# Seven block products for one more second product of a two-MoE kernel, with W_out's factors made while it is decoded

## The chip, the cores and the metric

The kernel runs on one core of a Trainium2 chip. The metric is the device time of one execution in microseconds; the time before is the median of three runs. Engines are called PE (TensorE: matmul, with PEld for its weight loads), DVE (VectorE), ACT (ScalarE), POOL (GpSimd) and SP (SyncE, which issues the DMAs).

## The reference

Windowed attention (4 batches, 8 heads, 576 positions, head size 64, window 128) gives x of 2304 tokens by 512. Two feed-forward blocks follow, called MoE here, each with its own W_in (512 by 2048) and W_out (2048 by 512):

```python
def _moe_ref(x, w_in, w_out):
    h = x @ w_in
    g = h * np.cos(h)
    return (g @ w_out).astype(np.float32)

def _moe2_ref(x, w_in, w_out):
    h = x @ w_in
    neg, pos = h <= -1.0, h >= 1.0
    g = np.where(pos, h, np.where(neg, 0.0, (h + 1.0) ** 2 / 4.0))
    return (g @ w_out).astype(np.float32)
```

All values are float32. The weights reach the chip as raw 64-bit words, which the kernel decodes to float32.

## The kernel before, in words

**Numbers.** Each float32 operand of a matmul is split in a high and a low part (`hi` by an ACT copy, `lo` by a DVE subtraction, `sub_lo`, L295). A product of two operands is three matmuls: high by high, high by low, low by high.

**Stages.** Attention runs first; its last rounds overlap the start of the first MoE. Tokens go in three chunks of 768, and a half chunk (384 columns, `HT`) is the width of most matmuls. The stages in PE's order are attention, then (0,0), (0,1), (0,2) of the first MoE and (1,0), (1,1), (1,2) of the second. In (0,0) weights are decoded as they are used (`first_weights`, L715).

**First products.** From (0,1) on, h = x·W_in is made by Strassen's scheme: seven block products in place of eight, for each of eight pairs p of 128-column blocks of W_in. The factors of W_in (A11, A12, S1 to S4, A22) are sums of its blocks, made once (`first_sums`, L339), stored to DRAM (`fd`) and loaded by each chunk (`stream`, L854). The factors of x (B11 to T4) are made by `prep` (L390). `product` (L866) is one block product, six matmuls of 384 columns. The PSUM results are joined: `snapshot` (L881) is an ACT copy out of a bank on which PE goes on adding, and `join` (L886) is a DVE add. `act` (L898) makes g of h.

**Second products, two ways.** In (0,1), (0,2) and (1,0) y = g·W_out is the classic eight block products: `contract` (L938) is six matmuls, called for 8 pairs, 2 halves and 4 blocks of 128 outputs, so 384 matmuls a chunk. W_out lies in SBUF as sixteen tiles `W` (`wo`), split in high and low. In (1,1) and (1,2) `deep` (L999) uses the seven products here as well: it first makes all h and g of the chunk (8 pairs, 7 products each), combines g's blocks (`combine`, L1067, four DVE subtractions for a pair), splits them (`halved`, L1055, seven a pair) and then runs 7 times 8 blocks (`block`, L1023) of six matmuls, 336 a chunk. The factors M1 to M7 of W_out come from DRAM (`fo`).

**Where W_out's factors come from, before.** `second_weights` (L686) decodes the second MoE's weights from 262 us on, a pair each 31 us. W_out's decoded tiles go to DRAM (`wd`, 16 stores of 256 KB). In (1,0) they are loaded again and split to the `wo` tiles (L1160 to L1166). From 520 us on `second_factors` (L977) stores M1, M2 and M4 from these tiles, loads W_out's pairs from `wd` a second time, makes the sums for M3, M5, M6 and M7 and stores them.

**PSUM in `deep`.** There are eight banks: two each in `ha` (a step's running cell, by p's parity), `hb` (M2's result and M4's), `cs` and `zs`. For each pair PE's order is M1(p), M7(p-1), M2(p), M4(p-1), M6(p), M3(p-1), M5(p), written by `step` (L1092) and the loop behind it. M1, M6 and M7 are summed on one bank with a snapshot behind each; M4 has a bank of its own and is joined with M7's snapshot.

**What orders the work.** PE's order is that in which the code issues it. For ACT, DVE, POOL and SP a planner (`Plan`, L106; `order`, L142) simulates the kernel with a table of operation lengths (`COST`, L58 to L72: the length for which the engine is held, and the latency until a successor may start), gives each operation a latest start from the PE order, and writes each engine's order out at compile time. `after=` holds an operation back to a planned time. Buffers with a `queue` name are handed out in the order of their rank. The chip then runs each engine's list in order, with semaphores.

Of the kernel before, what the change touches and what calls it, by code (L numbers as in the profile page):

```python
# [39 lines left out]
OUT_FROM, OUT_STEP = 520.0, 12.0  # L40
W2_FROM, W2_STEP = 262.0, 31.0
EARLY = 2
SUM_FROM, SUM_STEP = 175.0, 15.6
# [8 lines left out]
U_BUFS = 2  # L52
UP_BUFS = 2
# [52 lines left out]
class Plan:  # L106
# [35 lines left out]
    def order(self):  # L142
# [25 lines left out]
        for tag in ("Q", "split", "raw", "pair", "half"):  # L168
# [89 lines left out]
def attention_moe_moe_kernel(  # L258
# [19 lines left out]
    wd = [dram.tile([128, 512], F32, name=f"wd{f}") for f in range(NF)]  # L278
# [367 lines left out]
    def moes():  # L646
# [3 lines left out]
        wd_res = [Res() for _ in range(NF)]  # L650
        wo = [[None] * NF for _ in range(2)]
# [10 lines left out]
        plan = Plan({"s": S_BUFS, "Q": Q_BUFS, "B": 14, "W": NF, "ld": LD_BUFS, "wu": U_BUFS, "so": SO_BUFS, "up": UP_BUFS, "split": N_SPLIT},  # L662
# [23 lines left out]
        def second_weights():  # L686

            def load_and_decode(j, u, ap, after):
                raw = Buf("ld", lambda: two.tile([128, 512], mybir.dt.int64, tag="ld", name=nm("wst"), bufs=LD_BUFS), "raw")
                op("S", "512", lambda: SP.dma_start(raw.t, w2[j // 2, j % 2]), writes=[raw], after=after)  # L690
                decode(raw, u, ap)

            for p in range(NP):
                s = Buf("up", pair_tile, "pair")
                start = W2_FROM + W2_STEP * p
                for f in (2 * p, 2 * p + 1):
                    load_and_decode(2 * f, s, lambda s=s, f=f: half_u(s.t, f), start)
                    t = Buf("so", part_tile)
                    c, i = (slice(256, 512), 3) if f % 2 else (slice(0, 512), 0)
                    w = c.stop - c.start  # L700
                    op("A", f"hi{w}", lambda t=t, s=s, f=f, c=c, w=w: ACT.copy(t.t[:, 0, 0:w], half_u(s.t, f)[:, c]),
                       reads=[s], writes=[t])
                    op("D", f"tt{w}", lambda t=t, s=s, f=f, c=c, w=w: sub_lo(
                        DVE, t.t[:, 1, 0:w], half_u(s.t, f)[:, c], t.t[:, 0, 0:w]), reads=[s], writes=[t])
                    op("S", str(w), lambda t=t, p=p, i=i, w=w: move(fd[1][p][i], t.t[:, :, 0:w]),
                       reads=[t], writes=[fac[1][p][i]])
                    a = Buf("wu", lambda: two.tile([128, 512], F32, tag="wu", name=nm("wu"), bufs=U_BUFS), "half")
                    load_and_decode(2 * f + 1, a, lambda a=a: a.t, start)
                    op("S", "256", lambda a=a, f=f: SP.dma_start(wd[f], a.t), reads=[a], writes=[wd_res[f]])
                first_sums(op, 1, p, s, lambda: Buf("so", part_tile), lambda i, p=p: fac[1][p][i])  # L710
# [4 lines left out]
        def first_weights(j):  # L715
# [5 lines left out]
            if h:  # L721
                u = Buf("wu", lambda: two.tile([128, 512], F32, tag="wu", name=nm("wu"), bufs=U_BUFS))
                ap = lambda: u.t
                wo[0][f] = w = Buf("W", lambda: big("W", NF, "wo"))
            else:
                if f % 2 == 0:
                    wi_u[p] = Buf("W", lambda: big("W", NF, "up", F32, (128, 4, 256))) if f < 12 else Buf("up", pair_tile)
# [58 lines left out]
        def mm_b(i, f):  # L786
# [4 lines left out]
            def go():  # L791
# [3 lines left out]
                for d in range(KD):  # L795
                    s = slice(d * 128, d * 128 + 128)
                    for k, (a, x) in enumerate(((0, 0), (0, 1), (1, 0))):
                        PE.matmul(y_of[i][d], lhsT=wo[0][f].t[:, a, s], rhs=part(x),  # L798
# [3 lines left out]
            return op("PE", f"b{w}", go, reads=[wo[0][f], *gs], writes=[bank[t] for t in tags])  # L802
# [3 lines left out]
        def evict(m, c, y, d, o, w, res):  # L806
            e = "DA"[turn[0] % 2]
# [32 lines left out]
        depth = {"Q": Q_BUFS, "ld": LD_BUFS, "so": SO_BUFS, "up": UP_BUFS}  # L840
# [13 lines left out]
        def stream(m, ring=("Q",)):  # L854
            units = []
            for p in range(NP):
                units.append({})
                for i, names in enumerate(UNITS):
                    w = 256 * len(names)
                    b = ring_buf(ring, w=w)  # L860
# [37 lines left out]
        def act(m, h, res, keep=None, clip="D"):  # L898
# [11 lines left out]
            elif clip == "A":  # L910
                op("A", "hi384", lambda: ACT.activation(t.t, h.t, AF.Relu, bias=one_), reads=[res], writes=[t])
                op("A", "hi384", lambda: ACT.activation(t.t, t.t, AF.Relu, bias=two_, scale=-1.0), writes=[t])
# [25 lines left out]
        def contract(cell, tag, m, p, d, g, first, last):  # L938

            def go():  # L940
# [3 lines left out]
                for i in range(2):  # L944
                    w, (gh, gl) = wo[m][2 * p + i].t, g[i]
# [4 lines left out]
            return op("PE", "b384", go, reads=[wo[m][2 * p], wo[m][2 * p + 1], *g[0], *g[1]], writes=[bank[tag]])  # L950
# [19 lines left out]
        for p in range(EARLY, NP):  # L970
            s = Buf("up", pair_tile)
            load_sum(op, p, s, [ud_res[p]], SUM_FROM + SUM_STEP * p)
            first_sums(op, 0, p, s, lambda: Buf("so", part_tile), lambda i, p=p: fac[0][p][i])
        second_weights()
        fo_res = {name: [Res() for _ in range(NP)] for name in SECOND}

        def second_factors():  # L977

            def put(name, p, t, w, c):
                op("S", "256", lambda: move(fo[name][p // 2][:, p % 2], w()[:, :, c:c + 256]),  # L980
                   reads=[t], writes=[fo_res[name][p]], after=OUT_FROM)

            for p in range(NP):
                e, o = wo[1][2 * p:2 * p + 2]
                put("M1", p, e, lambda e=e: e.t, 0)
                put("M2", p, o, lambda o=o: o.t, 0)
                put("M4", p, o, lambda o=o: o.t, 256)
                s = Buf("up", pair_tile)
                for i in range(2):
                    op("S", "256", lambda s=s, i=i, p=p: SP.dma_start(half_u(s.t, i), wd[2 * p + i]),  # L990
                       reads=[wd_res[2 * p + i]], writes=[s], after=OUT_FROM + OUT_STEP * p)

                def store(f, t, p=p):
                    for k, name in enumerate((("M7", "M5"), ("M3", "M6"))[f]):
                        put(name, p, t, lambda t=t: t.t, 256 * k)

                sum_steps(op, s, lambda: Buf("so", part_tile), SECOND_SUMS, store)

        def deep(c, fills, bt, nxt, base):  # L999

            cs, zs = (("y3", "h1"), ("h0", "y1"))[::1 if c == 1 else -1]
            ha, hb = ("h2", "h3"), ("y2", "y0")
            ring = ("Q", "ld", "Q") if c == 1 else ("Q", "ld", "Q", "so", "Q", "up", "Q", "ld", "Q", "so", "Q", "up", "ld")
            units = stream(1, ring)
            right = {}
            for name in SECOND:
                right[name] = []
                for q in range(NP // 2):
                    b = ring_buf(ring, (128, 2, 2, 256))
# [82 lines left out]
            def step(name, p):  # L1092
                x = state.setdefault(p, {"a": Cell(), "b": Cell(), "b2": Cell(), "c": Cell()})
# [20 lines left out]
                elif name == "M7":  # L1114
                    mul("S3", x["a"], ta, "T3", False, True)
# [3 lines left out]
                elif name == "M4":  # L1119
                    mul("A22", x["b2"], hb[1], "T4", True, True)  # L1120
                    h = join(x["b2"], hb[1], x["u"])
                    act(1, h, h, (x["g", 1], 0))
                elif name == "M3":
                    mul("S4", x["c"], tc_, "B22", False, True)
                    h = join(x["c"], tc_, x["v"])
                    act(1, h, h, (x["g", 0], 1))
# [24 lines left out]
        for n, (m, c) in enumerate(((0, 1), (0, 2), (1, 0), (1, 1), (1, 2))):  # L1151
            ms, ys = sets[n % 2], sets[1 - n % 2]
            tb, tc_ = ms[2], ms[3]
            if (m, c) == (1, 1):
                second_factors()
            if m and c:
                fills, bt = deep(c, fills, bt, (1, 2) if c == 1 else None, 7 * NP * (c - 1))
                continue
            units = stream(m)
            if (m, c) == (1, 0):  # L1160
                for f in range(NF):
                    wo[1][f] = b = Buf("W", lambda: big("W", NF, "wo"))
                    u = Buf("wu", lambda: two.tile([128, 512], F32, tag="wu", name=nm("wu"), bufs=U_BUFS))
# [58 lines left out]
            nxt = {(0, 1): (0, 2), (0, 2): (1, 0), (1, 0): (1, 1), (1, 1): (1, 2)}.get((m, c))  # L1222
# [4 lines left out]
            if nxt:  # L1227
                bt = prep(op, *nxt, begun[1:2])
            for d in range(KD):
                y_block(0, NP - 1, d, g0[NP - 1], False, True)  # L1230
            if nxt:
                for p in range(2, NP - 1):
                    for d in range(KD):
                        y_block(1, p, d, t1(p), False, False)
# [60 lines left out]
```

## Time and profile before

| what | value |
|---|---|
| median of 3 runs | 856.46 us (856.1 to 857.72) |
| the profiled execution, its own time | 856.33 us |
| its span, first to last instruction | 854.5 us |
| instructions | 16042 |
| PE busy | 843.3 us, 99% of the span |
| DVE busy | 716.3 us, 84% |
| ACT busy | 643.1 us, 75% |
| POOL busy | 83.4 us, 10% |
| DMA | 241.71 MB, mean 283 GB/s |
| granted TensorE clock | 1.00 |

The table is read from the top: an engine that is busy for nearly the whole span sets the time, and what the others do matters where that engine waits for them. 1.8 us of the execution's own time lie outside of the span.

### The profile page before, as it was taken

What the parts mean: (1) busy time and instruction counts of PE and PEld (TensorE: products, weight loads), DVE (VectorE), ACT (ScalarE), POOL (GpSimd) and SP (SyncE); (2) the same over time, 40 slices, a digit from 0 to 9 for tenths busy, and PEclk for the clock granted to TensorE, in tenths of its full rate; (3) what the DMA queues carried; (4) which work ended last, traced back from release to release, by engine and by line L of the source; (5) the groups of instructions that cost most, each with busy time, mean ns of one, the idle gap of its engine ahead of it and who ended that gap; (6) DMA issues with size and microseconds to landing.
All of it is one profiled execution on the core that took longest, in us unless ns stands there. A gap on an engine that the chain in (4) does not pass through costs nothing.

```text
span 854.5 us, 16042 instructions
## 1 busy us (share of the span) xinstructions
PE 843.3 (99%) x5376; PEld 810.6 (95%) x5376; DVE 716.3 (84%) x1657; ACT 643.1 (75%) x1430; POOL 83.4 (10%) x118
## 2 busy tenths in 40 slices
PE   7999999999999999999999999999999999999998
PEld 5888888888899999999999999999999999999998
DVE  7999989899978989978888976877779999488954
ACT  7999898998867778678778677776478867488652
POOL 5878620000000000000000000000000000000000
PEclk9999999999999999999999999999999999999999
DMA  9868547677699999599879589998599999887861
GB/s 331 274 225 274 170 156 274 236 256 258 233 332 361 358 349 332 187 326 332 315 268 339 202 300 378 386 371 289 162 321 338 317 347 302 296 272 271 313 211 56
DMA packets 107730, 241.71 MB, mean 283 GB/s; under 512 B 10368, under 2 KB 57472, under 8 KB 107648
## 3 DMA queue, kind: packets, MB, share of 16 engines
q1 hardware_dynamic: 107648, 240.69, 80.2%
q8 instruction: 43, 0.70, 0.3%
q14 instruction: 39, 0.32, 0.1%
HBM read 174.59 MB, written 63.96 MB: 279 GB/s over the span
## 4 chain that ended last, share of the span: by engine, by line
PE 94%; DVE 2%; POOL 2%; issue 1%; ACT 0%; DMA 0%; POOLq 0%
PE h L875 34%; PE y L947 23%; PE y L1036 14%; PE h L759 8%; PE y L798 8%; PE pa L487 3%; PE pa L541 2%; PE pa L567 2%; POOL sc L524 2%; DVE sc L500 1%; ACT sc L505 0%; DMA qk<-in_qkv 0%; DVE pt L551 0%; DVE c L888 0%; DVE x L296 0%
## 5 line engine op out<-in xcount | busy, mean ns | idle before, releaser
L875 PE MATMUL h<-b,wq 128*128 128x384 f32 x1680 | 302.0, 334 | 0.6 <-ACT c L883 0.6
L875 PEld LDWEIGHTS h<-b,wq 128*128 128x128 f32 x1680 | 292.0, 188 | 1.0 <-ACT c L883 0.9
L947 PE MATMUL y<-gh,wo 128*128 128x384 f32 x768 | 203.4, 334 | 0.0
L947 PEld LDWEIGHTS y<-gh,wo 128*128 128x128 f32 x768 | 139.5, 188 | 0.0
L947 PE MATMUL y<-gl,wo 128*128 128x384 f32 x384 | 128.3, 334 | 0.0
L1036 PE MATMUL y<-gs,wq 128*128 128x384 f32 x672 | 118.1, 334 | 0.0
L1036 PEld LDWEIGHTS y<-gs,wq 128*128 128x128 f32 x672 | 116.6, 188 | 0.0
L888 DVE TENSOR_TENSOR c<-h,c 128x384 f32<-128x384 f32 x136 | 75.0, 554 | 39.9 <-ACT c L883 24.8
L883 ACT COPY c<-h 128x384 f32<-128x384 f32 x120 | 57.0, 475 | 50.8 <-PE h L875 49.6
L505 ACT ACTIVATE sc<-sc,up 128x256 f32<-128x256 f32 (+1 forms) x144 | 70.2, 489 | 11.8 <-DVE up L500 10.5
L1064 ACT CAST gs<-g 128x384 fp32r<-128x384 f32 x96 | 49.3, 514 | 34.5 <-PE y L1036 31.7
L524 POOL TENSOR_TENSOR sc<-sc,up 128x512 f32<-128x512 f32 (+1 forms) x71 | 70.8, 1018 | 22.0 <-DVE up L514 13.6
L947 PEld LDWEIGHTS y<-gl,wo 128*128 128x128 f32 x384 | 72.1, 188 | 0.0
L759 PE MATMUL h<-x,wi 128*128 128x512 f32 (+1 forms) x384 | 72.0, 337 | 0.0
L296 DVE TENSOR_TENSOR gs<-g,gs 128x384 fp32r<-128x384 f32 x96 | 53.2, 555 | 17.6 <-ACT gs L1064 17.1
L759 PEld LDWEIGHTS h<-x,wi 128*128 128x128 f32 x384 | 59.9, 190 | 8.0 <-issue 0.2
L500 DVE CUSTOM_DVE_ANT_0 sc<-pa,dist 128x256 f32<-128x256 f32 (+1 forms) x144 | 51.2, 401 | 5.6 <-PE pa L487 5.3
L908 ACT ACTIVATE t<-t,values 128x384 f32<-128x384 f32 x64 | 39.1, 616 | 11.5 <-DVE t L905 10.6
L296 DVE TENSOR_TENSOR so<-up,so 128x512 fp32r<-128x512 f32 x64 | 41.4, 652 | 3.4 <-ACT so L334 3.1
L680 DVE TENSOR_SCALAR wst<-wst 128x512 uint16<-128x512 uint16 x55 | 42.1, 770 | 1.5 <-ACT wst L672 1.2
L672 ACT ACTIVATE wst<-wst 128x512 int32<-128x512 uint16 x64 | 43.0, 674 | 0.0
L296 DVE TENSOR_TENSOR gl<-t,gh 128x384 fp32r<-128x384 f32 (+1 forms) x64 | 37.6, 587 | 6.4 <-ACT gh L894 4.3
(96 smaller groups left out, 1341.3 us busy)
## 6 DMA issues: line engine op xcount, KB each, us to landing
wq<-fd SPq DMA_DIRECT2D x120, 512.0 KB, 5.7
wst<-in_w SPq DMA_DIRECT2D x64, 512.0 KB, 5.0
wq<-foM SPq DMA_DIRECT2D x56, 512.0 KB, 5.6
fd<-so SPq DMA_DIRECT2D x40, 512.0 KB, 5.6
qk<-in_qkv SPq DMA_DIRECT2D x36, 320.0 KB, 5.1
wq<-fd SPq DMA_DIRECT2D x40, 256.0 KB, 5.3
foM<-so SPq DMA_DIRECT2D x32, 256.0 KB, 5.6
xs<-xd SPq DMA_DIRECT2D x40, 192.0 KB, 5.2
```

The source lines that it names most:

```text
L296: eng.tensor_tensor(out=out, in0=full, in1=f32(hi), op=ALU.subtract)
L500: maxes.append(used(op("D", f"max{w}", lambda j=j, h=h, c=c, w=w, at=at, sc=sc: DVE.tensor_tensor_reduce(out=sc.t[:, h, 0:w], in0=cells[j, ...
L505: exps.append(used(op("A", f"exp{w}", lambda h=h, c=c, w=w, sc=sc: ACT.activation(sc.t[:, h, 0:w], sc.t[:, h, 0:w], AF.Exp, bias=stats(p, ...
L524: used(op("P", f"norm{2 * w}", lambda sc=sc, j=j, w=w: POOL.tensor_tensor(out=sc.t[:, :, 0:w], in0=sc.t[:, :, 0:w], in1=stats(p, 8 + 2 * j ...
L759: PE.matmul(h, lhsT=wi[f].t[:, k, s], rhs=x, start=(n == 0), stop=(n == 11))
L798: PE.matmul(y_of[i][d], lhsT=wo[0][f].t[:, a, s], rhs=part(x), start=(f == 0 and k == 0 and not (i and d % 2)), stop=(f == NF - 1 and k == ...
L875: PE.matmul(cell.t, lhsT=unit.t[:, a, s], rhs=bs[kt].t[:, x, :], start=(start and i == 0), stop=(stop and i == 5), skip_group_check=True)
L883: op("A", "copy384", lambda: ACT.copy(s.t, cell.t), reads=[bank[tag]], writes=[s])
L888: op("D", "tt384", lambda: DVE.tensor_tensor(out=to.t, in0=cell.t, in1=s.t, op=ALU.add), reads=[bank[tag], s] if new else [bank[tag]], wri ...
L947: PE.matmul(cell.t, lhsT=w[:, a, s], rhs=x.t, start=(first and i == 0 and k == 0), stop=(last and i == 1 and k == 2), skip_group_check=True)
L1036: PE.matmul(cells[i].t, lhsT=w.t[:, k, a, i * 128:i * 128 + 128], rhs=g.t[x], start=(start and n == 0), stop=(stop and n == 2), skip_group ...
L1064: op("A", "hi384", lambda: ACT.copy(b.t[0], ap()), reads=[res], writes=[b])
```

## The change

The stage (1,0) now runs through `deep` like (1,1) and (1,2). The copies of W_out in DRAM (`wd`), its reload and its second split are gone. `second_weights` decodes in two sweeps: first W_in's pairs (from 235.7 us, one each 18 us) with their factors, then W_out's pairs (from 370.5 us, one each 16.6 us), whose factors M1 to M7 are made and stored at once. In the second MoE's weights every fourth extraction of the signs goes from DVE to ACT (`SIGN2`). In `deep` M4 adds on to the bank of M7, behind M7's snapshot, and `act` reads h from PSUM; the join is gone. All evictions of the first MoE's outputs are ACT's (`EV`). In (1,0) part of the stream uses `W` buffers (`LENT`). The pool `wu` is gone (the first MoE's use takes an `s` tile), `up` has three buffers for two. The planner's table changes for some lengths.

```diff
-OUT_FROM, OUT_STEP = 520.0, 12.0
-W2_FROM, W2_STEP = 262.0, 31.0
+OUT_FROM, OUT_STEP = 370.5, 16.6
+W2_FROM, W2_STEP = 235.7, 18.0
+SIGN2 = "DDDA"
+EV = "A"
+CLIP = "DD"
+LENT = ("Q", "W", "Q", "W"), ("Q", "W", "Q", "W"), ("Q", "Q", "Q", "Q")
-SUM_FROM, SUM_STEP = 175.0, 15.6
+SUM_FROM, SUM_STEP = 146.0, 14.2
-U_BUFS = 2
-UP_BUFS = 2
+UP_BUFS = 3
...
-          "tt384": (0.47, 0.62), "ts384": (0.47, 0.62), ..., "tt512": (0.7, 0.85), ..., "lo384": (0.53, 0.68), "ts16": (0.72, 0.82),
+          "tt384": (0.475, 0.72), "ts384": (0.47, 0.62), ..., "tt512": (0.62, 0.9), ..., "lo384": (0.48, 0.75), "ts16": (0.55, 0.95),
...
             def load_and_decode(j, u, ap, after):
...
-                decode(raw, u, ap)
+                decode(raw, u, ap, "", SIGN2[j % len(SIGN2)])
+
+            def part(u, f, lo, hi, names):
+                w = hi - lo
+                t = Buf("so", part_tile) if w == 512 else Buf("s", lambda: small("wp", F32R, (128, 2, 256)))
+                op("A", f"hi{w}", ...)
+                op("D", f"tt{w}", ...)
+                for dst, c, n, res in names:
+                    op("S", str(n), lambda dst=dst, c=c, n=n: move(dst(), t.t[:, :, c:c + n]), reads=[t], writes=[res])
...
+            for h in range(2):
+                for p in range(NP):
+                    e, o = 2 * p, 2 * p + 1
+                    start = (W2_FROM + W2_STEP * p, OUT_FROM + OUT_STEP * p)[h]
+                    s = Buf("up", pair_tile, "pair", start)
+                    for f in (e, o):
+                        load_and_decode(2 * f + h, s, lambda s=s, f=f: half_u(s.t, f), start)
+                        if not h and f == e:
+                            part(s, f, 0, 512, [(lambda p=p: fd[1][p][0], 0, 512, fac[1][p][0])])
+                        elif not h:
+                            part(s, f, 256, 512, [(lambda p=p: fd[1][p][3], 0, 256, fac[1][p][3])])
+                        elif f == e:
+                            part(s, f, 0, 256, [out_part("M1", p, 0)])
+                        else:
+                            part(s, f, 0, 256, [out_part("M2", p, 0)])
+                            part(s, f, 256, 512, [out_part("M4", p, 0)])
...
+                    sum_steps(op, s, lambda: Buf("so", part_tile), SECOND_SUMS, store)
...
         def evict(m, c, y, d, o, w, res):
-            e = "DA"[turn[0] % 2]
+            e = EV[turn[0] % len(EV)]
...
         def deep(c, fills, bt, nxt, base):
-            cs, zs = (("y3", "h1"), ("h0", "y1"))[::1 if c == 1 else -1]
-            ha, hb = ("h2", "h3"), ("y2", "y0")
-            ring = ("Q", "ld", "Q") if c == 1 else ("Q", "ld", "Q", "so", "Q", "up", "Q", "ld", "Q", "so", "Q", "up", "ld")
-            units = stream(1, ring)
+            cs, zs = (("y0", "y2"), ("h2", "h3"))[::-1 if c == 1 else 1]
+            ha, hb = ("h0", "y1"), ("h1", "y3")
+            ring = ("Q", "ld", "Q", "so", "Q", "up", "Q", "ld", "Q", "so", "Q", "up", "ld")
+            units = stream(1, ring) if c else stream(1, ("Q",), {p: LENT[(p > 5) + (p > 6)] for p in range(1, NP)})
...
                 elif name == "M7":
-                    mul("S3", x["a"], ta, "T3", False, True)
+                    mul("S3", x["a"], ta, "T3", False, False)
                     x["u"] = snapshot(x["a"], ta)
                     h = join(x["c"], tc_, x["u"], True)
                     act(1, h, h, (x["g", 1], 1), "A")
                 elif name == "M4":
-                    mul("A22", x["b2"], hb[1], "T4", True, True)
-                    h = join(x["b2"], hb[1], x["u"])
-                    act(1, h, h, (x["g", 1], 0))
+                    mul("A22", x["a"], ta, "T4", False, True)
+                    act(1, x["a"], bank[ta], (x["g", 1], 0), CLIP[0])
...
-            if (m, c) == (1, 1):
-                second_factors()
-            if m and c:
-                fills, bt = deep(c, fills, bt, (1, 2) if c == 1 else None, 7 * NP * (c - 1))
+            if m:
+                fills, bt = deep(c, fills, bt, (1, c + 1) if c < 2 else None, 7 * NP * c)
                 continue
             units = stream(m)
-            if (m, c) == (1, 0):
-                for f in range(NF):
-                    wo[1][f] = b = Buf("W", lambda: big("W", NF, "wo"))
-                    u = Buf("wu", ...)
-                    op("S", "256", lambda u=u, f=f: SP.dma_start(u.t, wd[f]), reads=[wd_res[f]], writes=[u, b])
-                    op("A", "hi512", lambda u=u, b=b: ACT.copy(b.t[:, 0, :], u.t), reads=[u], writes=[b])
-                    op("D", "tt512", lambda u=u, b=b: sub_lo(DVE, b.t[:, 1, :], u.t, b.t[:, 0, :]), reads=[u], writes=[b])
```

## Rows read from the trace of the kernel before

**Rows 1.** The page: its head and engines' busy time.

```profile
span 854.5 us, 16042 instructions
PE 843.3 (99%) x5376; PEld 810.6 (95%) x5376; DVE 716.3 (84%) x1657; ACT 643.1 (75%) x1430; POOL 83.4 (10%) x118
```

**Rows 2.** Windows: stretch, length, busy of PE, PEld, DVE, ACT, POOL (instructions); clock, DMA share, GB/s.

```profile
0.00:116.00 116.00, 108.66 (x1140) 91.16 (x1140) 104.09 (x428) 102.81 (x359) 83.39 (x118) 1.00 0.71 242
116.00:238.00 122.00, 122.00 (x707) 107.96 (x704) 110.71 (x206) 105.79 (x200) 0.00 (x0) 1.00 0.72 251
238.00:492.00 254.00, 253.43 (x1464) 252.60 (x1463) 221.64 (x445) 188.26 (x381) 0.00 (x0) 1.00 0.86 306
492.00:617.00 125.00, 125.00 (x723) 125.00 (x722) 92.66 (x190) 85.38 (x168) 0.00 (x0) 1.00 0.89 318
535.00:560.00 25.00, 25.00 (x146) 25.00 (x145) 18.65 (x40) 18.92 (x37) 0.00 (x0) 1.00 1.05 383
617.00:675.00 58.00, 58.00 (x337) 58.00 (x336) 49.82 (x110) 49.55 (x100) 0.00 (x0) 1.00 0.90 318
660.00:685.00 25.00, 25.00 (x147) 25.00 (x146) 24.02 (x54) 20.68 (x42) 0.00 (x0) 1.00 0.91 324
```

**Rows 3.** The chain that ended last: start, length, engine and line.

```profile
580.80 33.28 PE y L947 x192
622.40 52.00 PE h L875 x300
678.56 52.00 PE y L1036 x300
```

**Rows 4.** PE's waits: for whom, us in total, times, longest.

```profile
PE pa L487 <- DMA qk<-in_qkv: 4.1, 1, 4.1
PE h L875 <- ACT c L883: 0.6, 1, 0.6
```

**Rows 5.** Groups of instructions, matmuls of the second products: count, busy, mean ns.

```profile
L947 PE MATMUL y<-gh,wo 128*128 128x384 f32 x768 | 203.4, 334 | 0.0
L1036 PE MATMUL y<-gs,wq 128*128 128x384 f32 x672 | 118.1, 334 | 0.0
```

**Rows 6.** Timeline of DVE, back to back: start, length, line, operation.

```profile
460.92 0.55 DVE L905 SCALAR_TENSOR_TENSOR t<-c,k 128x384 f32<-128x384 f32 x1
461.38 0.68 DVE L296 TENSOR_TENSOR so<-up,so 128x512 fp32r<-128x512 f32 x1
461.99 0.75 DVE L680 TENSOR_SCALAR wst<-wst 128x512 uint16<-128x512 uint16 x1
462.53 0.58 DVE L934 TENSOR_TENSOR g<-c,t 128x384 f32<-128x384 f32 x1
...
478.41 0.42 DVE L330 TENSOR_TENSOR up<-up 128x256 f32<-128x256 f32 x1
478.74 0.76 DVE L680 TENSOR_SCALAR wst<-wst 128x512 uint16<-128x512 uint16 x1
```

**Rows 7.** Timeline at the start of (0,1): M5 and M7, M7's snapshot, M4.

```profile
245.95 2.25 PE L875 MATMUL h<-b,wq 128*128 128x384 f32 x12
248.24 0.48 ACT L883 COPY c<-h 128x384 f32<-128x384 f32 x1 [0.25 <-PE h L875]
248.77 0.45 PE L875 MATMUL h<-b,wq 128*128 128x384 f32 x1 [0.57 <-ACT c L883]
```

**Rows 8.** Timeline of ACT in (1,1): the snapshots of M1 and then M7.

```profile
630.76 0.48 ACT L883 COPY c<-h 128x384 f32<-128x384 f32 x1 [0.16 <-PE h L875]
631.13 0.62 ACT L919 ACTIVATE t<-t,values 128x384 f32<-128x384 f32 x1
631.80 0.48 ACT L883 COPY c<-h 128x384 f32<-128x384 f32 x1
```

**Rows 9.** Groups of instructions: M4's clip from PSUM, its square, ACT's sign extraction.

```profile
L916 DVE TENSOR_SCALAR t<-h 128x384 f32<-128x384 f32 x8 | 4.5, 557 | 6.3 <-PE h L875 6.3
L919 ACT ACTIVATE t<-t,values 128x384 f32<-128x384 f32 x48 | 29.4, 613 | 1.8 <-DVE t L916 1.8
L676 ACT ACTIVATE wst<-wst 128x512 f16<-128x512 f32 x9 | 12.4, 1376 | 0.0
```

More of the change, by code (lines that the diff above doesn't have):

```diff
@@ L167, in order @@
         queued, n_queue = {}, {}
-        for tag in ("Q", "split", "raw", "pair", "half"):
+        for tag in ("Q", "split", "raw", "pair"):
             queue = [(b.rank, place[o], o) for o in ops for b in o.new if b.queue == tag]
@@ L649, in moes @@
         fac = [[[Res() for _ in UNITS] for _ in range(NP)] for _ in range(2)]
-        wd_res = [Res() for _ in range(NF)]
-        wo = [[None] * NF for _ in range(2)]
+        wo = [None] * NF
         wi = [None] * NF
@@ L690, in load_and_decode @@
                 op("S", "512", lambda: SP.dma_start(raw.t, w2[j // 2, j % 2]), writes=[raw], after=after)
-                decode(raw, u, ap)
[L693 to L710, printed above, removed]
@@ new lines, in out_part, with store @@
+            def out_part(name, p, c):
+                return lambda: fo[name][p // 2][:, p % 2], c, 256, fo_res[name][p]
+            for h in range(2):
[14 more added lines that the diff above has]
+                            part(s, f, 256, 512, [out_part("M4", p, 0)])
+                    if not h:
+                        first_sums(op, 1, p, s, lambda: Buf("so", part_tile), lambda i, p=p: fac[1][p][i])
+                        continue
+                    def store(f, t, p=p):
+                        for k, name in enumerate((("M7", "M5"), ("M3", "M6"))[f]):
+                            dst, _, n, res = out_part(name, p, 0)
+                            op("S", "256", lambda t=t, k=k, dst=dst: move(dst(), t.t[:, :, 256 * k:256 * k + 256]),
+                               reads=[t], writes=[res])
+                    sum_steps(op, s, lambda: Buf("so", part_tile), SECOND_SUMS, store)
@@ L797, in go @@
                     for k, (a, x) in enumerate(((0, 0), (0, 1), (1, 0))):
-                        PE.matmul(y_of[i][d], lhsT=wo[0][f].t[:, a, s], rhs=part(x),
+                        PE.matmul(y_of[i][d], lhsT=wo[f].t[:, a, s], rhs=part(x),
                                   start=(f == 0 and k == 0 and not (i and d % 2)),
                                   stop=(f == NF - 1 and k == 2 and (i == 0 or d % 2 == 1)))
-            return op("PE", f"b{w}", go, reads=[wo[0][f], *gs], writes=[bank[t] for t in tags])
+            return op("PE", f"b{w}", go, reads=[wo[f], *gs], writes=[bank[t] for t in tags])
         turn = [0]
         def evict(m, c, y, d, o, w, res):
-            e = "DA"[turn[0] % 2]
+            e = EV[turn[0] % len(EV)]
             turn[0] += 1
@@ L852, in ring_buf, with stream @@
             return Buf(tag, make, "Q")
-        def stream(m, ring=("Q",)):
+        def stream(m, ring=("Q",), lent={}):
             units = []
@@ L970, in moes @@
         for p in range(EARLY, NP):
-            s = Buf("up", pair_tile)
+            s = Buf("up", pair_tile, "pair", SUM_FROM + SUM_STEP * p)
             load_sum(op, p, s, [ud_res[p]], SUM_FROM + SUM_STEP * p)
             first_sums(op, 0, p, s, lambda: Buf("so", part_tile), lambda i, p=p: fac[0][p][i])
+        fo_res = {name: [Res() for _ in range(NP)] for name in SECOND}
         second_weights()
[L975 to L997, printed above, removed]
         def deep(c, fills, bt, nxt, base):
-            cs, zs = (("y3", "h1"), ("h0", "y1"))[::1 if c == 1 else -1]
-            ha, hb = ("h2", "h3"), ("y2", "y0")
-            ring = ("Q", "ld", "Q") if c == 1 else ("Q", "ld", "Q", "so", "Q", "up", "Q", "ld", "Q", "so", "Q", "up", "ld")
-            units = stream(1, ring)
+            cs, zs = (("y0", "y2"), ("h2", "h3"))[::-1 if c == 1 else 1]
+            ha, hb = ("h0", "y1"), ("h1", "y3")
+            ring = ("Q", "ld", "Q", "so", "Q", "up", "Q", "ld", "Q", "so", "Q", "up", "ld")
+            units = stream(1, ring) if c else stream(1, ("Q",), {p: LENT[(p > 5) + (p > 6)] for p in range(1, NP)})
             right = {}
@@ L1220, in t1 @@
                 return g1[p]
[L1222 removed]
+            nxt = {1: (0, 2), 2: (1, 0)}[c]
             begun.clear()
```

48 lines of the change are left out of this document (20 added, 28 removed), and 4 rows, old and new, of the table COST.

## The prediction

> **What bounds the kernel now.** I read the page's head first: PE is busy in 843.3 of 854.5 us [rows 1]. That alone says little, since a busy PE need not run at its pace, so the stages come next. [...] The chain that ended last gives the pace: 192 matmuls of 384 columns take 33.28 us, and 300 take 52.00, which is 173.3 ns each, alike in the classic second product, in the seven first products and in the seven second ones [rows 3]. Among PE's waits only one of 0.6 us lies behind the attention [rows 4]. So in the stage that the change rewrites, PE's work is the time: a matmul less is 173.3 ns less, as long as DVE, ACT and the DMAs keep up.
>
> **What is removed from PE.** The classic second product of a chunk is 8 pairs x 2 halves x 4 blocks x 6 matmuls = 384 (the row of its high parts has 768, two thirds of the three chunks' 1152); the seven products are 7 x 8 x 6 = 336 (672 for two chunks) [rows 5]. The first product keeps its matmuls, and M4 only changes its bank. So 48 matmuls go: 48 x 0.1733 = **8.32 us**. [...]
>
> **What is added to DVE.** Back to back, DVE starts the next instruction 0.46 us after a 384-wide one, 0.61 after a 512-wide, 0.54 after a sign extraction, 0.33 after a 256-wide [rows 6]; the lengths shown overlap, so I use these steps.
>
> From 238 to 492 us (first MoE, chunks 1 and 2) come in: the sums for M3, M5, M6, M7, 8 x (4 x 0.33 + 2 x 0.61) = 20.3; the low parts for M1, M2, M4, 24 x 0.33 = 7.9; the last pair's decoding and W_in factors, which now cannot lie behind 492, at most 4 x (0.54 + 0.61) + 0.61 + 0.33 + 2.5 = 8.0. Out go eight sign extractions (4.3), eight evictions (3.7), and the first MoE's sums of two pairs, which start 30 to 40 us earlier (5.1). Net +23.1: DVE goes from 221.6 to 244.7 of 254 us, 96% [rows 2]. PE was unbroken beside a DVE at 91% over 122 us and at 96% over 25 us [rows 2], so this lies at the edge of what the trace shows. The cover is time: the factors are due only when the blocks begin, 56 products x 1.04 = 58 us into (1,0), so late decoding may run past 492.
>
> In these 58 us a pair costs DVE three joins, two clips, four products, four subtractions and M1's low part: 14 x 0.46 = 6.4 us in the 7.28 us of its seven products, 88%, with some 7 us left for late decoding. In (1,1) the old form needed one join more and had part of W_out's sums besides, and PE waited nowhere from 617 to 675 [rows 2]. In (1,1) and (1,2) each pair loses a join (0.46) and its clip reads PSUM, which can cost no more than the 0.56 of that form [rows 9]. I put DVE's load at no PE time.
>
> **ACT** takes in 238 to 492 eight sign extractions (11.0 at 1.376), and 16 + 24 copies and 8 evictions, at most 0.61 each [rows 9]: 40 us at most, into 65.7 idle [rows 2]. Nothing on PE's path. Its 24 further copies in (1,0), 15 us at most, meet 39.6 idle.
>
> **DMA and SP.** Gone are 48 transfers of 256 KB (`wd`), 12.6 MB; new are 28 loads of 512 KB of factors for (1,0), 14.7 MB. The 56 factor stores move from behind 520 us into 370 to 500: 238 to 492 rises from 77.7 MB by at most 14.7 - 4.2 = 10.5 to 88 MB, 347 GB/s, share 0.98. PE ran unbroken at 383 GB/s and 1.05 [rows 2], and the stream is loaded several tiles ahead. Cost 0. What would end this cover is a burst: SP issues in order, so a factor load that waits for its store holds the stream behind it.
>
> **What waits newly.** First, M4. In `deep` it had its own bank; now it must follow M7's snapshot, with only M2 of the next pair between. The same wait stands in the trace with nothing between: M7 ends at 248.20, the copy runs from 248.24 to 248.72, and M4 starts at 248.77, 0.57 us of PE idle [rows 7]. M2 fills 1.04 us, less the 0.16 by which a matmul's shown 334 ns exceed its pace, so 0.88: a slack of 0.31 us. In (1,1) M1's copy starts at 630.76, directly after PE's release, and M7's at 631.80, 1.04 later, which is when M7 ends: ACT was free [rows 8]. Bounds: 0, or 0.30 for each of 24 pairs (ACT just begun on a 0.61 instruction), 7.2 us. I take 0.03 a pair, 0.7 us, by [rows 8], which are this same place.
>
> Second, M1 two pairs on uses that bank again. Until then M4's h must be clipped, squared and compared: 0.56 + 0.61 + 0.58 [rows 6, 9], with 0.16 and four handovers of 0.05, 2.1 us, while PE has M6, M3 and M5, 3.12 us. If each of three hops met a running instruction in full, 1.5 us, the wait would be 0.5 a pair, 12 us; with half of each there is none. I take 0.3 us in all.
>
> **The first 238 us.** Other lengths give another list there, but its scores, exponentials and transposes keep theirs. PE idles 7.3 us before 116 [rows 2], 4.1 of it for the first load [rows 4]. At most 3.2 could be gained; lost could be as much. I take 0. The tail keeps its blocks: 0.
>
> **Sum.** The profiled execution took 856.33 us (span 854.5 and 1.8 around it): 856.33 - 8.32 + 0.7 + 0.3 = 849.0. The median of the runs is 0.13 above this execution, so **849.1 us**.
>
> **Rivals.** (B) The two waits cost part of the gain, 0.1 to 0.27 us a pair, 2.4 to 6.5 us: 850.5 to 854.7. For it: DVE and ACT at 85% or more in 617 to 675, three hops on one bank. Against: copies that start at once [rows 8].
>
> (C) DVE is the bound from 238 to 550. If its work exceeds my count by 17 us (9 idle before 492, some 7 behind), late factors stop the blocks, and another 8 us would eat the gain: 855 to 858. Against: 25 us is a tenth of the stretch.
>
> (D) Slower: M7's snapshot stands in ACT's list behind two instructions of another pair. Then M4 waits 2 x 0.51 - 0.31 = 0.7 us, 24 times, 17 us: 865. It turns slower where the mean wait passes 8.32 / 24 = 0.35 us, that is with ACT 0.66 us late on average. A lateness of ACT is then PE's, because nothing else may run. [...] The trace agrees: in [rows 7] PE stood still until the copy was done. Against (D): ACT idles 15% in this phase, and the planner knows this wait.
>
> (E) That the change doesn't do what it says would need the 48 matmuls back; the code leaves no room, so it has no chance of its own.
>
> **How the numbers follow.** The forecast, 847 to 850.5, has 0.58; B 0.24; C 0.07; D 0.11. A measurement of this kernel can tell about 0.2%, 1.7 us, from no change. The forecast and B are faster by more (below 854.7): 0.82. C lies around no change: 0.07. D is slower: 0.11. The range goes from 847.0 (the whole 8.32 and a third of the 3.2 us in the attention) to 854.7 (B's end) and leaves out 0.18.
>
> **What would show it.** Right: 5328 matmuls, 1008 of them in the seven second products; a pace of 173.3 ns in all long stretches; PE's waits behind 116 us under 2 us in sum; (1,0) some 116 us long, not 125; DVE near 96% and the DMAs near 0.98 in 238 to 492; no `wd` rows. Wrong: PE waits of 0.2 us or more for ACT's snapshot, or for DVE's product of M4, repeated every 7.28 us in `deep` (B, D); PE waits for factor loads or for split parts in the second half of (1,0) (C); PE idle above 9 us before 116.

## The result, and the profile after

The changed kernel takes 848.9 us against 856.63 us (medians); the ratio is 0.9913, with a 95% interval from 0.9893 to 0.9932. So it is faster by 0.9%, and 849.1 was forecast. (Three executions took 848.51, 848.91 and 850.49 us; a fourth of 1685.62 us was disturbed and is left out, and with it the median would be 849.7.) The profiled execution took 848.51 us, 7.82 less than that of before.

The page's head, after:

```profile
span 846.7 us, 16036 instructions
PE 835.2 (99%) x5328; PEld 801.7 (95%) x5328; DVE 728.3 (86%) x1689; ACT 671.6 (79%) x1484; POOL 83.4 (10%) x118
```

Against [rows 1] PE has 48 matmuls less and 8.1 us less of busy time, while DVE has 12 us more and ACT 28.5. The matmuls by group, after (line, tiles, count, busy, mean ns):

```profile
L1035 PE MATMUL y<-gs,wq 128*128 128x384 f32 x1008 | 177.4, 334 | 0.0
L969 PE MATMUL y<-gh,wo 128*128 128x384 f32 x512 | 135.6, 334 | 0.0
```

1008 is 3 x 336: all three chunks of the second MoE now have the seven second products [rows 5]. The chain that ended last, after (start, length, engine and line):

```profile
331.32 33.28 PE y L969 x192
456.12 33.28 PE y L969 x192
497.72 52.06 PE h L897 x300
553.94 52.00 PE y L1035 x300
614.26 52.00 PE h L897 x300
670.42 52.00 PE y L1035 x300
786.90 55.65 PE y L1035 x321
```

The same chain of the kernel before, its last row of matmuls:

```profile
795.04 55.65 PE y L1036 x321
```

The pace is still 33.28 / 192 = 52.00 / 300 = 173.3 ns [rows 3]. Here stands the whole account. The blocks of (1,1) begin at 670.42, before at 678.56: 8.14 us sooner. 8.32 would be the 48 matmuls; 0.12 was lost ahead of (1,0), and 0.06 in it (52.06 for 52.00), which leaves 8.14. From there to the end of the span it is 846.7 - 670.42 = 176.28 us, before 854.5 - 678.56 = 175.94: 0.34 more in the tail, so 7.80 for the span. The last row of matmuls still starts 8.14 us sooner (786.90 for 795.04) and is as long as before, so the 0.34 us lie behind PE. The last joins start 8.14 us sooner (842.58 for 850.72) and the last two stores are issued 8.13 us sooner (843.17 for 851.30): what is longer comes behind that issue.

PE's longest waits, after:

```profile
PE pa L489 <- DMA qk<-in_qkv: 4.1, 2, 3.8
PE pa L543 <- POOL sc L526: 2.8, 6, 0.7
PE h L897 <- ACT c L905: 0.6, 1, 0.6
```

Nothing new waits on PE: the one wait behind the attention is that of [rows 4], at the same place. The windows, after (stretch, length, busy of PE, PEld, DVE, ACT, POOL with their instructions, clock, DMA share, GB/s):

```profile
0.00:116.00 116.00, 108.66 (x1138) 90.61 (x1140) 104.13 (x429) 102.83 (x360) 83.41 (x118) 1.00 0.72 244
116.00:238.00 122.00, 122.00 (x708) 107.90 (x705) 112.73 (x217) 108.91 (x203) 0.00 (x0) 1.00 0.79 271
238.00:492.00 254.00, 253.43 (x1464) 252.60 (x1463) 232.97 (x482) 210.00 (x432) 0.00 (x0) 1.00 0.94 335
492.00:550.00 58.00, 58.00 (x337) 57.87 (x336) 50.55 (x107) 52.58 (x103) 0.00 (x0) 1.00 0.91 327
550.00:608.00 58.00, 58.00 (x336) 58.00 (x335) 49.18 (x100) 36.98 (x77) 0.00 (x0) 1.00 0.92 332
```

The moved work is seen beside [rows 2]: from 238 to 492 DVE rises from 221.64 to 232.97 us, ACT from 188.26 to 210.00, the DMAs from 306 to 335 GB/s, and PE loses nothing. Last, the stores of W_out's factors, which decide over the blocks (line, queue, DMA, count: ns of the issue, first and last start in us):

```profile
L305 SPq DMA_DIRECT2D foM<-so x32: 359/460/2349, 420.2 to 536.6; - x32
L305 SPq DMA_DIRECT2D foM<-wp x24: 319/383/1449, 385.3 to 516.8; - x24
```

The blocks that need them run from 549.8 us on, a pair's block each 1.04 us: M1's last at about 559, M6's last at about 575 (it is the 24th block, and the third stands at 553.94, where the continuous row begins).

### The profile page after: what moved, and what is told of

Its sections match the earlier page's. It is cut to its first block, busy times and chain, and to the rows that moved or that the text cites. A ratio compares the mean times of both kernels' runs of the same rounds, so it can differ in the third digit from the quotient of the medians.

```text
span 846.7 us, 16036 instructions
## 1 busy us (share of the span) xinstructions
PE 835.2 (99%) x5328; PEld 801.7 (95%) x5328; DVE 728.3 (86%) x1689; ACT 671.6 (79%) x1484; POOL 83.4 (10%) x118
## 4 chain that ended last, share of the span: by engine, by line
PE 94%; DVE 3%; POOL 2%; DMA 1%; issue 1%; ACT 0%; SPq 0%; POOLq 0%; DVEq 0%
PE h L897 34%; PE y L1035 21%; PE y L969 16%; PE h L781 8%; PE y L820 8%; PE pa L489 3%; PE pa L543 2%; PE pa L569 2%; POOL sc L526 2%; DVE sc L502 2%; DMA qk<-in_qkv 1%; DVE pt L553 0%; DVE c L910 0%; DVE up L516 0%; ACT ys L832 0%
## 5 line engine op out<-in xcount | busy, mean ns | idle before, releaser
L1035 PE MATMUL y<-gs,wq 128*128 128x384 f32 x1008 | 177.4, 334 | 0.0
L1035 PEld LDWEIGHTS y<-gs,wq 128*128 128x128 f32 x1008 | 175.0, 188 | 0.0
L969 PE MATMUL y<-gh,wo 128*128 128x384 f32 x512 | 135.6, 334 | 0.0
L1063 ACT CAST gs<-g 128x384 fp32r<-128x384 f32 x144 | 74.0, 514 | 46.7 <-PE y L1035 44.9
L298 DVE TENSOR_TENSOR gs<-g,gs 128x384 fp32r<-128x384 f32 x144 | 79.8, 555 | 21.9 <-ACT gs L1063 21.3
L969 PEld LDWEIGHTS y<-gh,wo 128*128 128x128 f32 x512 | 92.9, 188 | 0.0
L969 PE MATMUL y<-gl,wo 128*128 128x384 f32 x256 | 85.5, 334 | 0.0
L526 POOL TENSOR_TENSOR sc<-sc,up 128x512 f32<-128x512 f32 (+1 forms) x71 | 70.8, 1018 | 22.0 <-DVE up L516 20.3
L949 DVE TENSOR_TENSOR g<-c,t 128x384 f32<-128x384 f32 x72 | 39.6, 554 | 19.5 <-ACT t L941 10.7
L820 PE MATMUL y<-gh,wo 128*128 128x512 f32 x128 | 42.1, 390 | 0.0
L332 DVE TENSOR_TENSOR up<-up 128x256 f32<-128x256 f32 x96 | 39.6, 419 | 0.7
```

Source lines behind the costliest of these rows:

```text
L298: eng.tensor_tensor(out=out, in0=full, in1=f32(hi), op=ALU.subtract)
L526: used(op("P", f"norm{2 * w}", lambda sc=sc, j=j, w=w: POOL.tensor_tensor(out=sc.t[:, :, 0:w], in0=sc.t[:, :, 0:w], in1=stats(p, 8 + 2 * j ...
L820: PE.matmul(y_of[i][d], lhsT=wo[f].t[:, a, s], rhs=part(x), start=(f == 0 and k == 0 and not (i and d % 2)), stop=(f == NF - 1 and k == 2 ...
L969: PE.matmul(cell.t, lhsT=w[:, a, s], rhs=x.t, start=(first and i == 0 and k == 0), stop=(last and i == 1 and k == 2), skip_group_check=True)
L1035: PE.matmul(cells[i].t, lhsT=w.t[:, k, a, i * 128:i * 128 + 128], rhs=g.t[x], start=(start and n == 0), stop=(stop and n == 2), skip_group ...
L1063: op("A", "hi384", lambda: ACT.copy(b.t[0], ap()), reads=[res], writes=[b])
```

## The experiments

All are edits of the changed kernel, but for one of the kernel before. "The change" stands for it and its 848.9 us, the middle of the three executions above. Times are medians.

**M4 with its own bank again.** Does the new wait of M4 for M7's snapshot cost anything?

```diff
-                    mul("S3", x["a"], ta, "T3", False, False)
+                    mul("S3", x["a"], ta, "T3", False, True)
...
-                    mul("A22", x["a"], ta, "T4", False, True)
-                    act(1, x["a"], bank[ta], (x["g", 1], 0), CLIP[0])
+                    mul("A22", x["b2"], hb[1], "T4", True, True)
+                    h = join(x["b2"], hb[1], x["u"])
+                    act(1, h, h, (x["g", 1], 0), CLIP[0])
```

> The changed kernel, with M4 given its own PSUM bank and its join back, as before the change. Theory (M4's new wait for M7's snapshot is hidden under M2 and costs nothing): within 0.5 us of the changed kernel, some 849, with 24 DVE joins more (24 x 0.47 = 11 us of DVE). Rival (the shared bank costs a little at each pair, 0.1 us x 24): 2.4 us faster, some 846.5.

Measured: 848.39 us, ratio to before 0.9904 (0.9889 to 0.9918). That is the change within what can be told. Its chain in (1,0):

```profile
497.67 52.00 PE h L897 x300
```

This row took 52.06 in the change, so the wait cost at most 0.06 us there; in (1,1) and (1,2) the rows are 52.00 in both. The joins that come back are free too. The rival's 846.5 falls.

**M4 directly behind M7.** M2 of the next pair no longer stands between them.

```diff
                 turns = [new, old] if p < NP else [old, new]
+                if 1 <= p < NP:
+                    for fn in (new[0], old[0], old[1], new[1], new[2], old[2], new[3]):
+                        fn()
+                    continue
```

> The changed kernel, with M4 issued directly behind M7, so that M2 of the next pair no longer lies between; this holds for 7 pairs in each of 3 chunks. Theory (M2 is the cover, and bare the loop costs the 0.57 us seen at the start of the first chunk): 21 x 0.57 = 12.0 us slower than the changed kernel, some 861, with 21 more PE waits of 0.57 us for ACT's snapshot. Rival (the hidden wait is short, or the planner hides it by other means): within 2 us, and PE's waits stay under 3 us.

Measured: 866.98 us, ratio 1.0119 (1.0097 to 1.0140), 18.1 us more than the change where 12.0 were expected. PE's waits, then PEld's, in this kernel:

```profile
PE h L897 <- ACT c L905: 12.5, 22, 0.6
PEld h L897 <- ACT c L905: 19.5, 22, 0.9
```

Its chain:

```profile
510.04 7.57 PE h L897 x42
561.35 52.00 PE y L1035 x300
683.75 52.00 PE y L1035 x300
```

The 21 waits came as foretold (the 22nd is the old one), and PE's view shows 0.57 us of each. But from one chunk's blocks to the next it is 122.40 us, in the change 670.42 - 553.94 = 116.48: 5.92 us for seven waits, 0.85 each. PE's idle time leaves a part out: the 42 matmuls between two waits take 7.57 us, where the pace gives 42 x 0.1733 = 7.28, so each wait has 0.29 us beside the 0.57 shown as idle. PEld's 0.89 is nearer. So M2 is the cover that makes the new wait free, as the prediction said, and by this its slack is an estimated 1.04 - 0.85 = 0.19 us, not 0.31.

**The old lengths under the change.** The planner gets the table of before; nothing else is edited (`COST` of the kernel before in place of the new one).

> The changed kernel, planned with the table of operation lengths of the kernel before. Theory (PE is full and the lists of the other engines have room, so that another order of them changes nothing): within 1 us of the changed kernel, some 849 to 850. Rival (the denser stages need the truer lengths, since the old table holds DVE for 0.72 us on a sign extraction that takes 0.54 and 0.70 on a 512-wide one that takes 0.61, and puts off the late factors): 3 us or more slower, with PE waits between 492 and 610.

Measured: 904.4 us, ratio 1.0557 (1.0540 to 1.0574). My theory is wrong by 55 us. PE's longest waits:

```profile
PE y L1035 <- DMA wq<-foM: 38.3, 2, 21.6
PE h L781 <- ACT wi L754: 8.2, 1, 8.2
```

Windows of the same kernel:

```profile
238.00:492.00 254.00, 252.30 (x1461) 250.10 (x1460) 215.74 (x434) 192.50 (x393) 0.00 (x0) 1.00 0.87 302
550.00:610.00 60.00, 23.42 (x125) 22.72 (x123) 50.39 (x106) 40.76 (x77) 0.00 (x0) 0.73 0.62 201
```

The loads of the second MoE's raw weights, and the stores of the factors:

```profile
L691 SPq DMA_DIRECT2D wst<-in_w x32: 332/333/1060, 245.0 to 580.4; - x32
L305 SPq DMA_DIRECT2D foM<-so x32: 359/423/962, 494.9 to 606.8; - x32
```

The last factor is stored at 606.8, 70 us later than in the change, and PE's blocks wait for their loads, 38.3 us. Yet DVE is less busy from 238 to 492 than in the change, 215.74 against 232.97: it had time, and the lists gave it no decoding, since the last raw weights are loaded at 580.4 us where the change loads them at 484.7. PE idles for 37 of 60 us there. The granted clock is 0.73 in that stretch, and PE's busy time is 187 ns a matmul (23.42 us for 125) where the change has 173 from 550 to 608 (58.00 for 336); how much of that is the clock was not separated. The other wait, 8.2 us, stands between 116 and 238 us, in (0,0), where PE is busy for 113.81 of 122 us: it is part of the 55 us, but no matter of the late factors.

**The new lengths alone**, in the kernel before.

> The kernel before, planned with the table of lengths of the changed kernel. Theory (the gain is the 48 matmuls alone): 856.5, the same as before within 0.5 us. Rival (part of the gain comes from the lengths): 1 to 3 us faster.

Measured: 858.19 us, ratio 1.0021 (1.0012 to 1.0030). Both the theory's 0.5 us and the rival's gain are missed: the lengths by themselves cost some 2 us here. In the profile, which is of the slowest of the ten executions (860.41 us), one new wait of 1.2 us for ACT's snapshot stands between 238 and 367 us, where PE is busy for 127.22 of 129 us. So the lengths are no part of the gain, but its condition, as the run with the old lengths shows.

**Which lengths.** First those of the decoding alone (`sg512`, `tt512`, `ts16` as before the change), then those of the 384-wide operations alone (`tt384`, `lo384`). Only the entries that change are printed.

```diff
-"sg512": (1.11, 1.46)  "tt512": (0.62, 0.9)  "ts16": (0.55, 0.95)
+"sg512": (1.3, 1.45)   "tt512": (0.7, 0.85)  "ts16": (0.72, 0.82)
```

> The changed kernel, planned with the old lengths of three operations alone: the sign extraction on DVE (0.72 for 0.55), on ACT (1.30 for 1.11) and the 512-wide DVE operations (0.70 for 0.62). Theory (the planner puts off the decoding because it takes these operations, which are nearly all of the decoding, for longer than they are): most of the 55 us that the whole old table cost, 30 us or more slower, PE waiting for factor loads in (1,0). Rival (the lengths and latencies of the 384-wide operations on PE's path do it): within 5 us.

Measured: 907.36 us, ratio 1.0582 (1.0564 to 1.0600), last store at 612.0.

```diff
-"tt384": (0.475, 0.72)  "lo384": (0.48, 0.75)
+"tt384": (0.47, 0.62)   "lo384": (0.53, 0.68)
```

> The changed kernel, planned with the old lengths of the 384-wide DVE operations alone (latency 0.62 for 0.72; the low parts 0.53 held for 0.48). Theory (the decoding's lengths do it): within 5 us of the changed kernel. Rival (these do it): 30 us or more slower.

Measured: 874.27 us, ratio 1.0200 (1.0185 to 1.0215), last store at 583.6. The decoding's lengths explain the whole loss, as the theory said (8.5 us of it are again the wait in (0,0)), but the others alone cost 25 us, where it said 5 at most. The two don't add up. Each overstates the time for which some work holds DVE (a 384-wide operation takes 0.46 us of it, [rows 6], and `lo384` had 0.53), but each also shortens latencies. Which of the two loses the room was not separated.

**More work for DVE, known to the planner.** Each low part of M7, M5, M3 and M6's factors is written twice more, then five times more.

```diff
+                        for _ in range(2):
+                            op("D", "tt512", lambda: sub_lo(DVE, t.t[:, 1, :], half_u(s.t, f), t.t[:, 0, :]),
+                               reads=[s], writes=[t])
```

> The changed kernel, with each of the 16 subtractions that make the low parts of M7, M5, M3 and M6's factors repeated twice: 32 more 512-wide DVE instructions of 0.61 us, 19.5 us, between 370 and 540 us. The planner knows of them. Theory (DVE has room: 21 us idle from 238 to 492 and 7 from 492 to 550 in the changed kernel): within 1 us of the changed kernel, some 849. Rival (these stages are at DVE's edge already, since lists in fixed order cannot use every gap): 5 us or more slower, PE waiting for factor loads in (1,0).

> As before, with each subtraction repeated five times: 80 more instructions, 49 us of DVE. Theory (28 us of room before the blocks begin): 49 - 28 = 21 us too much, of which at most 9 fit behind 550; 10 to 25 us slower than the changed kernel, PE waiting for loads of late factors. Rival (room was far larger, DVE is no limit here): within 3 us.

Measured: 880.7 us for two, ratio 1.0278 (1.0252 to 1.0304), and 913.42 us for five, 1.0654 (1.0638 to 1.0670). The first was to be free and cost 32 us: the rival holds. The second was to cost 10 to 25 us and cost 64.5. Windows of the change, for comparison:

```profile
238.00:367.00 129.00, 128.43 (x743) 127.60 (x742) 116.20 (x238) 100.10 (x207) 0.00 (x0) 1.00 0.91 333
367.00:492.00 125.00, 125.00 (x723) 125.00 (x722) 116.77 (x245) 109.91 (x226) 0.00 (x0) 1.00 0.97 336
```

Windows with two repeats:

```profile
367.00:492.00 125.00, 125.00 (x723) 125.00 (x722) 117.92 (x242) 102.41 (x210) 0.00 (x0) 1.00 0.87 304
550.00:610.00 60.00, 38.23 (x200) 37.14 (x199) 56.92 (x115) 35.09 (x72) 0.00 (x0) 0.83 0.61 212
```

Its stores, and its longest wait of PE:

```profile
L305 SPq DMA_DIRECT2D foM<-so x32: 360/461/907, 426.5 to 596.2; - x32
```

```profile
PE y L1038 <- DMA wq<-foM: 21.8, 3, 16.6
```

With five, the window before the blocks' stage:

```profile
367.00:492.00 125.00, 125.00 (x723) 125.00 (x722) 117.84 (x238) 94.60 (x194) 0.00 (x0) 1.00 0.78 272
```

This pair shows where the room ends. The added work belongs to W_out's pairs, which are loaded from 370 us on (`OUT_FROM`), so none of it can go ahead of that: from 238 to 367 DVE is busy for 116 of 129 us in all three kernels. From 367 to 492 it is busy for 116.77 us in the change, 117.92 with 19.5 us more to do and 117.84 with 49 us more: these lists don't fill DVE beyond some 118 of 125 us. Nearly all that is added goes behind 492, where (1,0)'s own products leave DVE little (it is busy for 50.55 of 58 us in the change), and the last store slips from 536.6 to 596.2 and 613.4. The change stands about 1 us from that already. Whether decoding that starts sooner than 370 us could use the 13 us that DVE idles ahead of it was not tried.

**Signs and evictions back on DVE.** `SIGN2 = "D"`, `EV = "DA"`, as before the change: 8 x 0.54 + 8 x 0.46 = 8 us more for DVE.

> The changed kernel, with all sign extractions and half of the first MoE's evictions back on DVE, as before the change: some 8 us of DVE work more before 492. Measured so far: 19.5 us of DVE work more puts the last factor's store from 537 to 596 us, 3 us for each us, and costs 31 us. Theory (the store of the last pair's factors has a margin of some 26 us, since the 24th block that needs them is at 575 in the changed kernel and a store and a load take some 11; only what goes beyond is paid): the last store near 560, within 3 us of the changed kernel. Rival (there is no margin): 10 us or more slower.

Measured: 861.84 us, ratio 1.0059 (1.0040 to 1.0079), the last store at 586.4 and M2's and M4's at 557.7. Neither number of the theory holds: the store slips by 50 us, not 24, and 13 us are lost. Without these two small edits, which I had entered as relief only, no gain is left. A window of it:

```profile
367.00:492.00 125.00, 124.93 (x720) 124.34 (x719) 112.81 (x236) 96.17 (x202) 0.00 (x0) 1.00 0.88 306
```

DVE is busy for less of this stretch than in the change (112.81 for 116.77 us), though it has more to do. So it isn't an engine at its limit that is late here, but another list that leaves more of its work for later.

**The decoding due 40 us sooner**, with its old lengths. In the planner `o.late` of all operations of `second_weights` is lowered by 40.

> The changed kernel with the old lengths of the decoding (which alone made 907 of it), and in the planner the latest starts of all operations of the second MoE's weights set 40 us sooner. Theory (the planner put these off as not yet due while it took the other work for longer than it is; no engine is too slow for them): the last factor's store is back before 565 us, and the time comes back below 870, of which some 8 us are a wait at 200 us that this doesn't mend. Rival (the planned lists are full with the old lengths, and an earlier due time only moves the lateness to PE's own work): 890 or more.

Measured: 894.97 us, ratio 1.0447 (1.0426 to 1.0468). PE's longest waits:

```profile
PE h L900 <- DVE g L952: 20.3, 2, 18.0
PE h L784 <- ACT wi L757: 8.4, 1, 8.4
```

The theory of decoding that is merely put off falls. The factors come sooner (last store 589.7 for 612.0), but now the products of (1,0) wait for DVE's own part of them, 20.3 us. So with the old lengths a different rank alone only chooses who is late. That the planned lists are full is the likely reason, but it is not shown: on the chip DVE is busy for 212.57 of the 254 us before 492, and other start times for the loads were not tried with the old lengths.

**Fewer matmuls in a stage of blocks.** M6's blocks in (1,0) (`short`) keep only their high by high part (32 matmuls are left out).

```diff
-                        for n, (a, x) in enumerate(((0, 0), (0, 1), (1, 0))):
+                        for n, (a, x) in enumerate(((0, 0), (0, 1), (1, 0))[:1 if short else 3]):
```

> The changed kernel, with the 8 blocks of M6 in (1,0) cut to high by high, so 32 matmuls are left out there. Theory (PE alone sets the pace of the blocks, and each matmul left out gives 173.3 ns): 5.5 us faster than the changed kernel, some 843.3. Rival (splits of 0.47 us on DVE, 0.42 on ACT, or the factor loads are as slow as the blocks): less than 2.8 us faster.

Measured: 844.21 us, 4.7 less than the change. The chain:

```profile
554.39 46.45 PE y L1036 x268
609.16 52.00 PE h L897 x300
```

From the blocks to the next chunk's products it is 54.77 us, in the change 60.32: 5.55 less, which is 32 x 0.1733. PE is the bound here after the change as well; that a matmul left out of this stage is worth its 173.3 ns is shown. (The blocks begin 0.45 us later than in the change, 554.39 for 553.94, so a little of it is lost ahead of them.)

**The one old wait.** In the first pair of (0,1) nothing stands between M7 and M4 [rows 7].

```diff
-        order = ("M1", 0, "M2", "M6", 1, "M5", "M7", "M4", "M3")
+        order = ("M1", 0, "M2", "M6", "M5", "M7", 1, "M4", "M3")
```

> The changed kernel, with the order of the first pair of (0,1) changed so that the second leftover block of the chunk before stands between M7 and M4, and M5 between M6 and M7. This takes away the one wait of 0.57 us for ACT behind the attention. Theory (a wait shown as 0.57 us costs 0.85, as the 21 such waits did): 0.85 us faster than the changed kernel, the wait gone from the profile, and all later stages 0.85 us sooner. Rival (M7 now waits for M6's snapshot instead): no difference, a wait of another length in its place.

Measured: 850.13 us, ratio to before 0.9926 (0.9913 to 0.9938), so no faster than the change. The wait at this place is gone, without the rival's wait for M6's snapshot in its place, and its stretch is full:

```profile
238.00:367.00 129.00, 129.00 (x752) 128.49 (x751) 115.27 (x236) 99.78 (x208) 0.00 (x0) 1.00 0.91 333
```

Its chain at the start of (0,1), ahead of (1,0) and behind its products:

```profile
241.41 2.76 PE y L820 x12
...
456.75 7.64 PE y L969 x44
...
556.37 52.00 PE y L1035 x300
```

In the change these stand at 239.94, 456.12 and 553.94. The execution is 1.47 us late at the first, which comes from the attention (below), 0.63 at the second, so 0.84 us were gained between, as expected; and 2.43 at the third: 1.80 us were lost again around the start of (1,0). PEld's waits from 230 to 620 us, all of them behind 456, where the change has none:

```profile
PEld h L897 <- ACT c L905: 0.7, 1, 0.7
PEld y L969 <- DVE gl L298: 0.6, 2, 0.4
PEld h L897 <- DVE g L949: 0.4, 2, 0.2
PEld y L969 <- ACT gh L916: 0.2, 1, 0.2
```

These sum to 1.9 us and took the gain. The order of one pair made the planner write other lists for the rest; the last store moved from 536.6 to 575.3. But for the kernel that leaves matmuls out, no version of these beats the change beyond what can be told.

## Why the prediction was right, and where it was not

**The 48 matmuls** gave 8.32 us, as worked out: the account above closes to 0.02 us (7.80 for the span, 7.82 measured for the execution), and the M6 run shows the same price a second time.

**The two new waits** were put at 1.0 us and cost 0.06 at most. The mechanism of the first is shown from both sides: free with M2 between, 0.85 us bare. The term's bare size was too small, as 0.57 was PE's shown idle time. Rival B's mechanism therefore is there and was fully covered; D's too, since 21 bare waits made the kernel slower than before, at 866.98. The 0.94 us put here and not spent are more than the 0.46 lost ahead of (1,0) and in the tail, so the 849.0 reckoned for the profiled execution lies near its 848.51 partly because small misses cancel.

**"I put DVE's load at no PE time"** came true, on a margin that I had sized wrongly. I reckoned DVE up to 244.7 of 254 us; it took 232.97, and 13 of the 56 factor stores ran behind 492, the last at 536.6. I then gave it 9 us of idle time before 492 and 7 behind, so that rival C needed 17 us of excess to begin and another 8 to eat the gain. With more work in the same lists DVE came no further than some 118 of the 125 us before 492, where the change has 116.8 already: C begins at once, and 19.5 us cost 32. With signs and evictions back, some 8 us, it stopped at 112.8 and 13 us were lost all the same, so the limit is no fixed figure of the engine; it depends on the lists that the planner finds. The chip ran the lists of the change as planned: in its trace DVE's 1689 instructions, ACT's 1484 and SP's 628 issues start in the planned order, kernel line by kernel line. C's mechanism was right (late factors stop the blocks), its threshold was not, and its 0.07 was too little for how near it lay. That the term came out at nothing is in part luck: it holds for the lists that these lengths and reliefs gave, and the prediction had looked at none of them.

**"Other lengths give another list there … I take 0"** is the weakest step, though not in the number that it gave. I priced the table for the first 238 us alone, where 0.12 us changed, and nowhere for the stages that it serves. The same edit with the old table would have been slower than before, 904.4 against 856.26 us. That the lists are planned with lengths near the real ones ([rows 6]: 0.61, 0.54, 0.46) lets DVE carry the moved work here. The idle DVE in the run with the old table shows that it is the list and not the engine that was late there. Which of its entries would do with a few hundredths less is open, since the two groups don't add up; so is whether other start times (`W2_FROM`, `OUT_FROM` and their steps) would serve the old table, since all runs keep those of the change.

**ACT and the DMAs** were as bounded: 210.0 us for at most 228, 335 GB/s and a share of 0.94 for 347 and 0.98. No new wait of PE for either is in the profile. **The tail** cost 0.34 us where I took 0; it lies behind the issue of the last store, and why is open.

## What to carry to other kernels

Where one engine is full and the trace shows its pace, work taken off it is worth that pace (here 173.3 ns a matmul: 8.32 us for 48, 5.55 for 32), and the question is whether the helpers' lists have room: an engine that idles for 6% of a stretch, in lists of fixed order, may have no usable room left there (here DVE, with some 118 of 125 us). Where a planner writes the lists, its table is part of the change: take the times from start to start of a busy engine, not the shown lengths (0.46 us for 0.55 to 0.58 on a 384-wide DVE operation [rows 6]), look at the lists that come out, and test by adding a little work to the fullest helper. A wait on PE should be costed by the distance of what stands around it, or by PEld's idle time, not by PE's (here 0.85 us by the distance, 0.89 by PEld, 0.57 by PE).

## What was not expected of the hardware

Executions of one kernel differ by some 2 us (before: 855.93 to 858.28 in one comparison). One profile shows 1.47 us of such a difference in the attention. Windows from 8 to 16 us, of the change:

```profile
8.00:12.00 4.00, 2.19 (x19) 1.31 (x16) 3.68 (x21) 3.84 (x18) 2.33 (x4) 1.00 1.05 405
12.00:16.00 4.00, 4.00 (x46) 3.25 (x45) 3.98 (x17) 2.85 (x12) 2.56 (x5) 1.00 1.05 401
```

and of the run with the other first pair:

```profile
8.00:12.00 4.00, 2.59 (x18) 1.63 (x14) 3.67 (x23) 4.00 (x20) 2.21 (x3) 1.00 1.05 407
12.00:16.00 4.00, 3.93 (x20) 3.09 (x22) 2.71 (x9) 1.55 (x8) 2.21 (x5) 0.57 1.05 401
```

In the run with the other first pair the granted clock is 0.57 from 12 to 16 us, and PE gets through 20 matmuls where the change has 46. PE had been idle for 1.4 of the 4 us before; but in the change it idled for longer there, 1.8 us, and the clock held, so what made it fall is open. That execution is 1.47 us late at 240 us. So differences under 2 us between two profiles are to be taken from the stages, not from the totals.
